# Longformer attention with two MLPs, one core: score banks filled up front, and new constants in the kernel's planner

## The chip, the cores and the metric

The kernel runs on one core of one Trainium2 chip. The metric is device time in microseconds (us), the median of several executions. TensorE is called PE here, VectorE DVE, ScalarE ACT, GpSimd POOL and SyncE SP.

## What is computed

```python
# local attention: 4 batches, 8 heads, 512 local and 32 global tokens, head size 64, window 32
s_ll = where(mask, scale * q_l @ k_l.T, -1e9)
out_l = sm(concat([scale * q_l @ k_g.T, s_ll])) @ concat([v_g, v_l])
out_g = sm(scale * q_g @ k_all.T) @ v_all
x = concat([out_g, out_l], axis=2)          # to [4*544 = 2176, 512]
h = x @ w_in                                # first MLP: 512 to 2048 to 512
x = (h * clip(h + 3, 0, 6) / 6) @ w_out
h = maximum(maximum(x @ w1, x @ w2), x @ w3)  # second MLP: 512 to 768 to 512
out = h @ w_out2
```

All of it is in float32. The large products split each operand into a high and a low part and make three products of them.

## The kernel before

The whole program is one list of steps. Each step (`op(...)`) names its engine, a cost in us, a due time, what it reads and writes and, for loads, the size in KB. `Plan.order()` walks a model of the chip, always taking the step that can start first (or, among those that can start within 0.02 us, the one due first), and writes the instructions out in the order found. On the chip every engine runs its instructions in that order, each waiting for its inputs; the planned times are not kept by anything. So a changed constant in the planner changes the order of instructions on PE, DVE, ACT, POOL and in SP's queue, and nothing else.

Attention runs per batch and pair of heads: `pair(b, pr, s0)`, 16 of them. The start `s0` of a pair, from which its due times count, grows by `STEPS[b]`. One pair loads Q, K (288 and 400 KB) and V (1024 KB) into rings of three buffers, makes the scores in two banks (L469: 64 small products), row maxima on DVE (L482), exponentials on ACT (L488), transposes (`flip`, L512), copies (L435), the product with V (`pv`, L523, output bank `o`), the division by the sums (L531), a second transpose (`xflip`, L538) and the split into high and low parts (`x_hi`, `x_lo`). Every second pair is followed by `globals_`, the attention of the global tokens (L576 to L628).

A score bank is not written everywhere by its scores, so each bank is first written whole by a product of ones, a *fill* (L419). Before, `full` holds six fills (four score banks, banks 6 and 7); the first scores wait for them, and the fifth score bank is filled after the first half of pair 0's scores.

Beside attention, 16 blocks of `w_in` are loaded through two buffers (`raw`, L664) and decoded on ACT, DVE and POOL (`decode`, `join`, L642 to L669). The first MLP's products (`first`, L695) fill PE's time between the steps of attention, as far as the attention output and the decoded weights are there. After the attention stage come the other products (L859, L983, L1138), with their own loads.

The planner's model has these terms that the change touches. Code for PE arrives in blocks of 256 instructions, the first border at `FIRST = 191`; when a border is passed, the next block but one is reckoned to arrive after `LATE` plus `SHARED` times the backlog of loads, at most 4 us. After an idle time of over 2 us, PE's steps count longer for 4 us (`cold`). A load of `kb` takes its turn in one pipe of 340 KB per us and lands 1.8 us later. `LOOK` says how far ahead the planner looks in sharing steps between ACT, DVE and POOL. `LAG` sets how early the weight loads of later stages may start.

In the last stage (L1120 and on), `single` and `double` take one or two blocks of 128 tokens. A `double` loads h twice (L1150, 384 KB, rows of 128 words), makes four sums of them on DVE or POOL (`wsum`, L677), splits them (L1160 and L677) and runs seven products through `quad` (L983), in which a copy of the first product's bank on ACT or DVE (`take`, L435) stands ahead of the third product.

Of the kernel before, what the change touches and what calls it, by code (L numbers as in the profile page):

```python
# [16 lines left out]
ALU = mybir.AluOpType  # L17
# [82 lines left out]
class Plan:  # L100
# [40 lines left out]
    def order(self):  # L141
# [15 lines left out]
        count, border, there, loads, cold = 0, FIRST, 0.0, [], -1e9  # L157
# [37 lines left out]
        while len(out) < len(self.ops):  # L195
            picks, wait, at = [], {}, {}
            for e, ops in cand.items():
                f = free.get(e, 0.0)
# [3 lines left out]
            for e, ops in cand.items():  # L202
# [5 lines left out]
                t0 = min(t for t, _ in ts)  # L208
# [21 lines left out]
            if o.eng == "PE":  # L230
                if FORM.get(o.what, "F") != form:
                    form = FORM.get(o.what, "F")
                    us += TURN
                if t - free.get("PE", 0.0) > 2.0 and t > COLD:
                    cold = t + 4.0
                if t < cold:
                    us += min(us, (cold - t) / 2)
                count += o.ni
                if count > border:
                    at_ = t + us * (1 - (count - border) / o.ni)  # L240
                    wait_ = max(0.0, there - at_)
                    at_, us = at_ + wait_, us + wait_
                    if wait_ > 0.2:
                        self.stalls.append((round(at_, 1), round(wait_, 1)))
                    if wait_ > 2.0:
                        cold = at_ + 4.0
                    behind = max([p - at_ for i, p in loads if i <= at_] + [0.0])
                    there, border = at_ + LATE + min(4.0, SHARED * behind), border + 256
# [30 lines left out]
COLD = 6.0  # L279
SPLIT = 2  # L280
LATE, SHARED = 2.473, 0.718
TS = "BC"
STEPS = (7.62, 8.87, 11.397, 7.881)
LAG = 124.236
# [4 lines left out]
LOOK = 1.25  # L289
# [6 lines left out]
def body(ctx, tc, q_n, k_n, v_r, w_in, w_o, w_3, w_4, out):  # L296
# [128 lines left out]
    full = [filled(bank) for bank in (*sbanks[:4], banks[6], banks[7])]  # L425
# [15 lines left out]
    def pair(b, pr, s0):  # L441
# [7 lines left out]
        for n, (t, src, cut, size) in enumerate(((Q, q_n, 256, NQ + SG), (K, k_n, 448, NK))):  # L449
            for i, (a, z) in enumerate(((0, cut), (cut, size)) if first_ else ((0, size),)):  # L450
                e, issue = ("ACT", nc.scalar) if first_ and n else ("SP", nc.sync)
                op(e, 0.45, lambda t=t, src=src, a=a, z=z, issue=issue: issue.dma_start(
                    out=t()[:, a:z], in_=src[b, pr][:, a:z]), s0 - 7.919 + i, w=[(t, i)] if first_ else [t],
                   kb=(z - a) / 2, rel=s0 - 15.079, what="qk"[n])
        op("SP", 0.5, lambda: nc.sync.dma_start(out=V(), in_=v_r[b, pr]), s0 - 4.432 + 5 * first_, w=[V], kb=1024, rel=s0 - 2.826, what="v")

        TB, NM, OB = [Buf(T["t"]) for _ in range(2)], Buf(T["nm"]), Buf(T["o"])
        for u, tiles in enumerate(((0, 1), (2, 3)) if first_ else (range(4),)):
# [18 lines left out]
            if not full[6:]:  # L477
                full.append(filled(sbanks[4], [head]))
# [27 lines left out]
        for hh in range(2):  # L506
            FB, pt = Buf(T["f"]), Buf(T["pt"])
            PT.append(pt)

            def flip(hh=hh, FB=FB):  # L510
                for i in range(4):
                    nc.tensor.transpose(FB()[:, 128 * i:128 * i + 128], TB[hh]()[:, i], ident)  # L512

            op("PE", 0.48, flip, s0 + 5.696 + hh, r=[(TB[hh], i) for i in range(4)], w=[FB, Buf(T["turn"])], what="flip", ni=8.2)
            op(AD, (0.585, 0.65), lambda e, pt=pt, FB=FB: copy(e, pt(), FB()), s0 + 5 + hh, r=[FB], w=[pt], what="flipped")
# [10 lines left out]
        op("PE", 0.95, pv, s0 + 3.515, r=PT + [V], w=[OB], what="pv", ni=129)  # L526
# [13 lines left out]
        op("PE", 0.48, xflip, s0 + 12.171, r=[OX], w=[XT], what="xflip", ni=8)  # L540
# [15 lines left out]
    def globals_(b, pr, g0):  # L556
# [7 lines left out]
        for a, ks in enumerate((GKEYS[0:2], GKEYS[2:3])):  # L564
# [14 lines left out]
            op("PE", (0.68, 0.3)[a], g_scores, g0 + 0.455, r=[Z[k] for Z in R for k in "QK"], w=[sg, (tg, "held")], what="g_scores", ni=8 * len(ks))  # L579
# [19 lines left out]
        for n, cs in enumerate((range(0, 4), range(4, 6))):  # L599
# [9 lines left out]
            op("PE", 0.11 * len(cs), g_flip, g0 + 3.512, r=[tg], w=[fb, Buf(T["turn"])], what="g_flip", ni=2 * len(cs))  # L609
# [13 lines left out]
        op("PE", 0.72, g_pv, g0 + 9.996, r=pts_g + [Z["V"] for Z in R], w=[og], what="g_pv", ni=96)  # L623
# [57 lines left out]
    def first(p, gs_, due):  # L681
# [28 lines left out]
        for g in gs_:  # L710
            store(p, g, Q[g], 0, 3, due)
            for a, b, o in ((3, 2, 2), (1, 3, 3), (1, 2, 1), (0, 1, 0)):
                op(DP if p in TS else "POOL", dp(n) if p in TS else pool(n), lambda e="POOL", g=g, o=o, a=a, b=b: tt(
                    e, q(g, o), q(g, a), q(g, b), ALU.subtract), due + 44.537, r=[(Q[g], a), (Q[g], b)], w=[(Q[g], o)], what="tsum",
                   two=True)
            store(p, g, Q[g], 3, 4, due)
# [9 lines left out]
    s = 4.158  # L726
    due1 = 40.0
    late = []
    for b in range(B + 1):
        if b < B:  # L730
            for pr in range(H // 2):
# [5 lines left out]
                if pr % 2:  # L737
                    late.append((b, pr, s + 3.453))
# [3 lines left out]
        if b == 0:  # L742
            for f in (g + NG * a for g in range(NG) for a in range(2)):
                src = w_in[:, f * 128:f * 128 + 128].rearrange("(k p) m -> p k m", p=128)
                k = 2 * (f % NG) + f // NG
                wi[f] = decode(src, "w", 22.156 + 1.579 * k, 11.396 + 1.115 * k)
# [344 lines left out]
    for p, i in (("P1", 0), ("R", 1), ("P2", 2), ("P3", 3), ("P5", 4), ("P6", 7), ("P7", 5), ("P4", 6)):  # L1091
# [3 lines left out]
           r=[(w4k, (k, i // 4)) for k in range(3)], w=[X4], kb=384, what="w4load", rel=TE - 30 - LAG)  # L1095
# [22 lines left out]
    def single(t0, due, t):  # L1118
# [4 lines left out]
        for i in range(2):  # L1123
            op("SP", 0.5, lambda i=i: nc.sync.dma_start(out=hl_()[:, i], in_=hd[:, 3 * i:3 * i + 2, t0:t0 + 128]), t - 20,
               r=rows(t0, (3 * i, 3 * i + 1)), w=[(hl, i)], kb=128, what="hload", rel=TE - 30 - LAG)
# [19 lines left out]
    def double(ts, due, t):  # L1145
# [3 lines left out]
        for i in range(2):  # L1149
            op("SP", 0.5, lambda i=i: nc.sync.dma_start(  # L1150
                out=blk(2 - 2 * i, 2).rearrange("p (k m) -> p k m", k=NH), in_=hd[:, :, ts[i]:ts[i] + 128]),
               t - 12, r=rows(ts[i]), w=[(W, 1 - i)], kb=384, what="hload")
# [76 lines left out]
```

## Time and profile before

| | us |
|---|---|
| median of 3 runs | 711.16 |
| lowest and highest | 710.18, 717.23 |
| profiled execution: time | 716.01 |
| profiled execution: span of the core | 714.2 |
| PE busy in the span | 696.9 (98%) |
| DVE, ACT, POOL busy | 526.7, 381.1, 128.9 |
| mean granted clock of PE | 0.993 |

The profile is of one execution, whose time is 1.8 us above its span. In the views, each line of a timeline has a start, a duration, the engine, the line of the kernel and the operation with its tiles; in brackets stands the idle time of the engine just before it and what ended that. A group "x64" is 64 instructions in a row.

### The profile page before, as it was taken

How to read it: one execution, taken by the hardware profiler on the slowest of the kernel's cores; microseconds unless marked ns; L12 is line 12 of the kernel's file. 1: busy time of each engine (PE TensorE's matmuls, PEld its weight loads, DVE VectorE, ACT ScalarE, POOL GpSimd, SP SyncE). 2: the span in 40 equal slices, each digit the busy share in tenths (PEclk: the TensorE clock that was granted, in tenths of full speed). 3: DMA queues.
4: the chain of work that ended last, by engine and by line, in shares of the span. 5: the costliest groups of instructions: out<-in, count | busy, mean ns of one | idle time of the engine just before them, and what ended most of it. 6: DMA issues, size and time to landing. Idle time of an engine off the chain costs nothing.

```text
span 714.2 us, 16046 instructions
## 1 busy us (share of the span) xinstructions
PE 696.9 (98%) x6380; PEld 619.8 (87%) x6380; DVE 526.7 (74%) x1114; ACT 381.1 (53%) x808; POOL 128.9 (18%) x163
## 2 busy tenths in 40 slices
PE   8799999999999999999999999999999999998998
PEld 5577878778888999988999998898999999997998
DVE  4688986657964575699867589998887876575781
ACT  6789887654332334565554366744454344254452
POOL 2137464200001343001010000011301320021210
PEclk9999999999999999999999999999999999999999
DMA  8599998715884765776576598001463371276542
GB/s 321 203 325 336 351 331 327 279 63 206 299 302 204 253 254 173 276 242 184 145 233 185 144 295 293 1 1 59 162 207 131 137 256 39 77 223 193 147 151 89
DMA packets 73147, 144.57 MB, mean 202 GB/s; under 512 B 4976, under 2 KB 43632, under 8 KB 70000
## 3 DMA queue, kind: packets, MB, share of 16 engines
q1 hardware_dynamic: 72784, 143.13, 59.0%
q8 instruction: 50, 0.82, 0.5%
q10 hardware_dynamic: 288, 0.41, 0.2%
q14 instruction: 25, 0.20, 0.1%
HBM read 98.04 MB, written 45.48 MB: 201 GB/s over the span
## 4 chain that ended last, share of the span: by engine, by line
PE 87%; DMA 6%; ACT 3%; DVE 2%; issue 1%; SPq 0%; POOL 0%; ACTq 0%; DVEq 0%
PE bank L983 33%; PE bank L695 23%; PE bank L859 22%; DMA raw<-in_w_in_dram 2%; DMA kr<-in_kn_dram 2%; PE o L523 1%; PE s L512 1%; PE s L469 1%; PE bank L1138 1%; DMA vr<-in_v_dram 1%; PE s L576 1%; PE s L620 1%; ACT t L488 1%; PE s L538 1%; DMA out_dram<-rf 1%
## 5 line engine op out<-in xcount | busy, mean ns | idle before, releaser
L695 PE MATMUL bank<-rx,rw 128*128 128x512 f32 (+1 forms) x960 | 198.0, 362 | 0.4 <-DVE rx L552 0.2
L695 PEld LDWEIGHTS bank<-rx,rw 128*128 128x128 f32 x960 | 161.7, 188 | 23.7 <-issue 1.2
L859 PE MATMUL bank<-rr,rw 128*128 128x320 f32 (+2 forms) x912 | 154.9, 331 | 0.7 <-DVE rr L677 0.6
L859 PEld LDWEIGHTS bank<-rr,rw 128*128 128x128 f32 x912 | 140.2, 188 | 14.8 <-DVE rr L677 1.8
L983 PE MATMUL bank<-rw,rr 128*128 128x256 f32 (+2 forms) x648 | 100.2, 302 | 0.1
L983 PEld LDWEIGHTS bank<-rw,rr 128*128 128x128 f32 x648 | 90.6, 188 | 5.0 <-ACT rf L435 0.7
L782 ACT CAST rr<-fw 128x1024 fp32r<-128x1024 f32 (+2 forms) x76 | 62.1, 820 | 53.6 <-PE bank L859 45.8
L677 DVE TENSOR_TENSOR rr<-fw,rr 128x1024 fp32r<-128x1024 f32 (+2 forms) x76 | 72.8, 964 | 23.6 <-ACT rr L782 22.8
L705 ACT ACTIVATE rq<-bank,three 128x512 f32<-128x512 f32 (+1 forms) x60 | 37.9, 635 | 48.6 <-PE bank L695 40.5
L677 POOL TENSOR_TENSOR rf<-rf 128x256 f32<-128x256 f32 (+2 forms) x34 | 34.3, 1020 | 142.6 <-DVE rf L652 40.8
L435 ACT COPY rf<-bank 128x256 f32<-128x256 f32 (+2 forms) x72 | 33.0, 465 | 47.6 <-PE bank L983 37.2
L707 DVE SCALAR_TENSOR_TENSOR rq<-rq,bank 128x512 f32<-128x512 f32 (+1 forms) x60 | 36.8, 618 | 29.1 <-ACT rq L705 28.7
L488 ACT ACTIVATE t<-t,nm 128x128 f32<-128x128 f32 x128 | 50.0, 394 | 13.4 <-DVE nm L482 13.2
L677 POOL TENSOR_TENSOR rq<-rq 128x256 f32<-128x256 f32 (+2 forms) x44 | 37.5, 853 | 108.3 <-DVE rq L677 82.4
L983 PE MATMUL bank<-rw,re 128*128 128x256 f32 (+2 forms) x369 | 54.4, 292 | 2.1 <-DVE bank L435 2.1
L983 PE MATMUL bank<-re,rr 128*128 128x512 f32 x222 | 54.9, 391 | 0.0
L983 PEld LDWEIGHTS bank<-rw,re 128*128 128x128 f32 x369 | 49.5, 188 | 3.7 <-DVE bank L435 2.3
L1077 DVE TENSOR_TENSOR rf<-rf,bank 128x320 f32<-128x320 f32 (+2 forms) x72 | 37.1, 530 | 14.3 <-PE bank L983 13.1
L983 PEld LDWEIGHTS bank<-re,rr 128*128 128x128 f32 x222 | 40.7, 188 | 8.0
L677 DVE TENSOR_TENSOR rf<-rf 128x256 f32<-128x256 f32 (+4 forms) x54 | 29.2, 572 | 7.2 <-DMA rf<-hd 7.1
L482 DVE CUSTOM_DVE_ANT_0 t<-s,mask 128x128 f32<-128x128 f32 x116 | 26.5, 285 | 10.6 <-PE s L469 10.6
L677 DVE TENSOR_TENSOR re<-rf,re 128x1024 fp32r<-128x1024 f32 (+4 forms) x20 | 26.5, 1330 | 3.9 <-ACT re L1160 3.9
(134 smaller groups left out, 970.2 us busy)
## 6 DMA issues: line engine op xcount, KB each, us to landing
vr<-in_v_dram SPq DMA_DIRECT2D x16, 1024.0 KB, 7.9
fw<-gsB SPq DMA_DIRECT2D x28, 512.0 KB, 4.8
raw<-in_w_dram SPq DMA_DIRECT2D x24, 512.0 KB, 3.9
fw<-gsC SPq DMA_DIRECT2D x28, 320.0 KB, 3.6
raw<-in_w_in_dram SPq DMA_DIRECT2D x16, 512.0 KB, 6.1
raw<-in_w_o_dram SPq DMA_DIRECT2D x16, 512.0 KB, 4.9
fw<-gsA SPq DMA_DIRECT2D x28, 256.0 KB, 2.9
gsB<-rq SPq DMA_DIRECT2D x6, 1024.0 KB, 5.1
```

The lines of the kernel that those rows point to most:

```text
L435: (nc.scalar.copy if eng == "ACT" else nc.vector.tensor_copy)(out=out, in_=in_)
L469: nc.tensor.matmul(SB[hh]()[QB * c:QB * c + QB, 128 * i + a:128 * i + z], lhsT=Q()[64 * hh:64 * hh + 64, QB * j:QB * j + QB], rhs=K()[64 * ...
L482: nc.vector.tensor_tensor_reduce(out=TB[hh]()[:, i], in0=SB[hh]()[:, 128 * i:128 * i + 128], in1=mask()[:, (i + 1) // 2 if i < 3 else 2], ...
L488: nc.scalar.activation(out=t, in_=t, func=ACTF.Exp, scale=-1.0, bias=NM()[:, 0, i, hh:hh + 1], accum_out=NM()[:, 1, i, hh:hh + 1])
L677: ENG[e].tensor_tensor(out=out, in0=a, in1=b, op=f)
L695: nc.tensor.matmul(ps()[:, 0:m], lhsT=w[:, i, k], rhs=xs(c)[:, j, k], start=(k == 0 and s == 0), stop=(k == KC - 1 and s == 2))
L705: op("ACT", us, lambda ps=ps, m=m, out=out: nc.scalar.activation(out=out(), in_=ps()[:, 0:m], func=ACTF.Relu, bias=three), -100, r=[ps], w ...
L707: op("DVE", us, lambda ps=ps, m=m, out=out: nc.vector.scalar_tensor_tensor(out=out(), in0=out(), scalar=6.0, in1=ps()[:, 0:m], op0=ALU.min ...
L782: op("ACT", act(n) + 0.01, lambda: nc.scalar.copy(out=out(0), in_=src()), due, r=r, w=[(w, "hi")], what=what + "_hi")
L859: nc.tensor.matmul(A[e]()[:, 0:n], lhsT=w[:, 2 * fp + f, u, e], rhs=r[:, v, f], start=(seed is None and fp + f + s == 0), stop=(fp == 3 an ...
L983: nc.tensor.matmul(bank()[:, 0:n], lhsT=w[:, u, k], rhs=r[:, v, k], start=(start and k + s == 0), stop=(k == K - 1 and s == 2), skip_group ...
L1077: op("DVE", dve(n), lambda q=q, src=src, mv=mv: nc.vector.tensor_tensor(out=mv(q)(), in0=mv(q)(), in1=src(), op=ALU.max), -200, r=[bank], ...
```

## The change

Seven fills (all five score banks and banks 6 and 7) stand ahead of the first scores, and the one behind them is gone. After the second half of pair 0's scores, two fills (`WARMERS = 2`) write the output bank `o`. In the planner, PE's steps except fills count up to double before 6.3 us (`cold` starts at `WARM`). The loads of w4 count as 500 KB instead of 384, those of h as 170 instead of 128 and as 560 instead of 384; the transfers themselves are the same. `LATE`, `SHARED`, `STEPS`, `LAG`, `LOOK` and the due and release times of Q, K, V, `flip`, `pv`, `xflip`, the global steps, the sums of the first MLP and the `w_in` loads have new values (those not in the excerpt: `g_scores` g0 + 0.455 to g0 + 0.071, `g_flip` g0 + 3.512 to g0 + 1.943, `g_pv` g0 + 9.996 to g0 + 5.183, the sums of the first MLP due + 44.537 to due + 48.004, the first s0 4.158 to 4.347, `globals_` s + 3.453 to s + 2.278). `COUNTED` is read nowhere in the diff.

```diff
-        count, border, there, loads, cold = 0, FIRST, 0.0, [], -1e9
+        count, border, there, loads, cold = 0, FIRST, 0.0, [], WARM
...
-                if t - free.get("PE", 0.0) > 2.0 and t > COLD:
+                if t - free.get("PE", 0.0) > 2.0 and t > WARM:
                     cold = t + 4.0
-                if t < cold:
+                if t < cold and o.what != "fill":
                     us += min(us, (cold - t) / 2)
...
-COLD = 6.0
+COUNTED = True
+WARM = 6.3
+WARMERS = 2
 SPLIT = 2
-LATE, SHARED = 2.473, 0.718
+LATE, SHARED = 2.304, 0.75
 TS = "BC"
-STEPS = (7.62, 8.87, 11.397, 7.881)
-LAG = 124.236
+STEPS = (7.844, 8.631, 11.405, 7.492)
+LAG = 127.749
...
-LOOK = 1.25
+LOOK = 0.745
...
-    full = [filled(bank) for bank in (*sbanks[:4], banks[6], banks[7])]
+    full = [filled(bank) for bank in (*sbanks, banks[6], banks[7])]
...
-                    out=t()[:, a:z], in_=src[b, pr][:, a:z]), s0 - 7.919 + i, w=[(t, i)] if first_ else [t],
-                   kb=(z - a) / 2, rel=s0 - 15.079, what="qk"[n])
-        op("SP", 0.5, lambda: nc.sync.dma_start(out=V(), in_=v_r[b, pr]), s0 - 4.432 + 5 * first_, w=[V], kb=1024, rel=s0 - 2.826, what="v")
+                    out=t()[:, a:z], in_=src[b, pr][:, a:z]), s0 - 12.857 + i, w=[(t, i)] if first_ else [t],
+                   kb=(z - a) / 2, rel=s0 - 14.853, what="qk"[n])
+        op("SP", 0.5, lambda: nc.sync.dma_start(out=V(), in_=v_r[b, pr]), s0 - 2.183 + 5 * first_, w=[V], kb=1024, rel=s0 - 3.098, what="v")
...
-            if not full[6:]:
-                full.append(filled(sbanks[4], [head]))
+            if first_ and u:
+                op("PE", 0.43 * WARMERS, lambda: [fill(OB()) for _ in range(WARMERS)], -100, after=[head], w=[OB], what="fill", ni=2 * WARMERS)
...
-            op("PE", 0.48, flip, s0 + 5.696 + hh, r=[(TB[hh], i) for i in range(4)], w=[FB, Buf(T["turn"])], what="flip", ni=8.2)
+            op("PE", 0.48, flip, s0 + 3.7 + hh, r=[(TB[hh], i) for i in range(4)], w=[FB, Buf(T["turn"])], what="flip", ni=8.2)
...
-        op("PE", 0.95, pv, s0 + 3.515, r=PT + [V], w=[OB], what="pv", ni=129)
+        op("PE", 0.95, pv, s0 + 2.373, r=PT + [V], w=[OB], what="pv", ni=129)
...
-        op("PE", 0.48, xflip, s0 + 12.171, r=[OX], w=[XT], what="xflip", ni=8)
+        op("PE", 0.48, xflip, s0 + 13.261, r=[OX], w=[XT], what="xflip", ni=8)
...
-                wi[f] = decode(src, "w", 22.156 + 1.579 * k, 11.396 + 1.115 * k)
+                wi[f] = decode(src, "w", 21.856 + 0.897 * k, 12.183 + 0.519 * k)
...
-           r=[(w4k, (k, i // 4)) for k in range(3)], w=[X4], kb=384, what="w4load", rel=TE - 30 - LAG)
+           r=[(w4k, (k, i // 4)) for k in range(3)], w=[X4], kb=500, what="w4load", rel=TE - 30 - LAG)
...
-               r=rows(t0, (3 * i, 3 * i + 1)), w=[(hl, i)], kb=128, what="hload", rel=TE - 30 - LAG)
+               r=rows(t0, (3 * i, 3 * i + 1)), w=[(hl, i)], kb=170, what="hload", rel=TE - 30 - LAG)
...
-               t - 12, r=rows(ts[i]), w=[(W, 1 - i)], kb=384, what="hload")
+               t - 12, r=rows(ts[i]), w=[(W, 1 - i)], kb=560, what="hload")
```

## Rows read from the trace of the kernel before

**Rows 1.** Busy time by stretch: us, engines, granted clock, DMA share, GB/s.

```profile
0.00:158.70 158.70, 147.40 (x3033) 116.03 (x3034) 113.43 (x464) 118.16 (x389) 56.19 (x96) 0.98 0.80 285
158.70:650.00 491.30, 490.43 (x2887) 445.92 (x2886) 375.70 (x597) 235.73 (x377) 65.51 (x63) 1.00 0.55 183
650.00:714.20 64.20, 59.09 (x464) 57.82 (x462) 37.58 (x53) 27.19 (x44) 7.24 (x4) 0.97 0.48 148
...
7.85:11.65 3.80, 3.75 (x76) 2.84 (x78) 1.80 (x11) 2.36 (x13) 0.20 (x1) 0.57 1.00 401
21.60:25.40 3.80, 3.68 (x65) 3.25 (x69) 2.16 (x6) 0.91 (x4) 0.00 (x0) 0.55 0.37 142
...
659.30:664.20 4.90, 4.89 (x28) 0.65 0.53 155
```

**Rows 2.** PE in order of time, 0 to 8 us: start, us, what.

```profile
1.05 1.89 PE L419 MATMUL s<-ones 128*128 128x512 bf16 x4 [1.05 <-DVE ones L318]
...
4.10 1.04 PE L469 MATMUL s<-kr,qr 64*32 64x96 f32 x32 [0.31 <-DMA kr<-in_kn_dram]
...
5.07 0.39 PE L419 MATMUL s<-ones 128*128 128x512 bf16 x1
...
5.39 0.65 PE L469 MATMUL bank<-kr,qr 64*32 64x128 f32 x32
...
7.90 1.59 PE L469 MATMUL s<-kr,qr 64*32 64x96 f32 x64 [1.86 <-DMA kr<-in_kn_dram]
```

**Rows 3.** PE's stops for issue, products before, and DMA queues from 18 us.

```profile
0.00:18.20 18.20, 14.76 (x348) 0.91 0.90 322
...
21.72 0.43 PE L523 MATMUL o<-vr,pt 128*32 128x64 f32 x15 [3.64 <-issue]
...
144.50 0.75 PE L620 MATMUL s<-vr,pt 128*32 128x64 f32 x35 [0.83 <-issue]
...
q8 instruction: 1, 0.02, 1.7%
```

**Rows 4.** SP's waits for w_in buffers, busy time by stretch, one PE wait.

```profile
SPq L664 <- DVE rq L652: 27.5, 7, 13.5
...
25.00:30.00 5.00, 4.66 (x177) 3.72 (x171) 4.17 (x14) 3.81 (x10) 0.80 (x2) 0.96 0.03 8
30.00:120.00 90.00, 87.20 (x1690) 69.19 (x1683) 74.58 (x287) 76.76 (x242) 43.91 (x58) 1.00 0.93 331
...
41.27 0.33 PE L512 MATMUL s<-ident,t 128*128 128x128 f32 x1 [1.26 <-ACT t L488]
```

**Rows 5.** V loads: median to landing, one issue, and its pv on PE.

```profile
vr<-in_v_dram SPq DMA_DIRECT2D x16, 1024.0 KB, 7.9
...
57.04 0.50 SPq L455 DMA_DIRECT2D vr<-in_v_dram  x1
...
65.32 1.10 PE L523 MATMUL o<-vr,pt 128*32 128x64 f32 x64 [0.31 <-DMA vr<-in_v_dram]
```

**Rows 6.** All engines in order of time, 654 to 660 us.

```profile
654.21 1.22 SPq L1150 DMA_DIRECT2D rf<-hd  x2
...
654.97 2.29 PE L983 MATMUL bank<-rw,re 128*128 128x256 f32 x18
...
656.83 2.09 DVE L677 TENSOR_TENSOR rf<-rf 128x384 f32<-128x384 f32 x4 [4.98 <-DMA rf<-hd]
...
658.84 0.42 DVE L435 COPY bank<-bank 128x256 f32<-128x256 f32 x1
...
659.31 1.51 PE L983 MATMUL bank<-rw,re 128*128 128x256 f32 x9 [2.06 <-DVE bank L435]
```

**Rows 7.** Loads by line: count, KB each, median us to landing.

```profile
rf<-hd SPq DMA_DIRECT2D x14, 384.0 KB, 4.6
...
rf<-w4d SPq DMA_DIRECT2D x8, 384.0 KB, 5.7
...
raw<-in_w_dram SPq DMA_DIRECT2D x24, 512.0 KB, 3.9
```

More of the change, by code (lines that the diff above doesn't have):

```diff
@@ L577, in g_scores @@
                                          tile_position=(0, 64 * m))
-            op("PE", (0.68, 0.3)[a], g_scores, g0 + 0.455, r=[Z[k] for Z in R for k in "QK"], w=[sg, (tg, "held")], what="g_scores", ni=8 * len(ks))
+            op("PE", (0.68, 0.3)[a], g_scores, g0 + 0.071, r=[Z[k] for Z in R for k in "QK"], w=[sg, (tg, "held")], what="g_scores", ni=8 * len(ks))
             for x, (_, at) in enumerate(ks):
@@ L607, in g_flip @@
                     nc.tensor.transpose(fb()[0:rows_g, 128 * j:128 * j + 128], tg()[:, at:at + rows_g], ident)
-            op("PE", 0.11 * len(cs), g_flip, g0 + 3.512, r=[tg], w=[fb, Buf(T["turn"])], what="g_flip", ni=2 * len(cs))
+            op("PE", 0.11 * len(cs), g_flip, g0 + 1.943, r=[tg], w=[fb, Buf(T["turn"])], what="g_flip", ni=2 * len(cs))
             e = ("ACT", "DVE")[n]
@@ L621, in g_pv @@
                                          start=(c == 0), stop=(c == 5), tile_position=(0, x))
-        op("PE", 0.72, g_pv, g0 + 9.996, r=pts_g + [Z["V"] for Z in R], w=[og], what="g_pv", ni=96)
+        op("PE", 0.72, g_pv, g0 + 5.183, r=pts_g + [Z["V"] for Z in R], w=[og], what="g_pv", ni=96)
         gx, xt = Buf(T["gx"]), Buf(T["s"])
@@ L713, in first @@
                 op(DP if p in TS else "POOL", dp(n) if p in TS else pool(n), lambda e="POOL", g=g, o=o, a=a, b=b: tt(
-                    e, q(g, o), q(g, a), q(g, b), ALU.subtract), due + 44.537, r=[(Q[g], a), (Q[g], b)], w=[(Q[g], o)], what="tsum",
+                    e, q(g, o), q(g, a), q(g, b), ALU.subtract), due + 48.004, r=[(Q[g], a), (Q[g], b)], w=[(Q[g], o)], what="tsum",
                    two=True)
@@ L723, in store @@
            r=[(Q, j) for j in range(k)], w=[(gk, (p, g, at))], kb=k * n / 2, what="gstore")
-    s = 4.158
+    s = 4.347
     due1 = 40.0
@@ L737, in body @@
                 if pr % 2:
-                    late.append((b, pr, s + 3.453))
+                    late.append((b, pr, s + 2.278))
                 s += STEPS[b]
```

## The prediction

> **What bounds the kernel now.** I read the span by stages first, because one share of busy time hides three different stages [rows 1]. In the attention stage (to 158.70 us) TensorE (PE) works 147.40 us, so it idles 11.30; in the middle, to 650 us, it idles 0.87; in the last 64.20 us it idles 5.11. PE is therefore the bound throughout, and a change of order can only win idle time or time at the lower clock. Almost all of both lies in three places. From 7.85 to 11.65 us the granted clock averages 0.57, from 21.60 to 25.40 it averages 0.55, and from 659.30 to 664.20 it averages 0.65, each time right after an idle stretch; a stretch at 0.5 runs at 1.2 GHz instead of 2.4 [rows 1]. The time that it costs is length times (1 - clock): 3.80 x 0.43 = 1.6 us, 3.80 x 0.45 = 1.7 us and 4.90 x 0.35 = 1.7 us.
>
> The second view is PE's own order of time at the start [rows 2], to see what each idle stretch waits for; the third is the place where PE stands without a visible cause [rows 3]; the fourth the loads and who holds SyncE's (SP's) queue [rows 4, 5]; the last is the gap near the end, engine by engine [rows 6].
>
> The sum is made against the profiled execution, 714.2 us of span and 716.01 us of time. The median of the runs shown is 711.16, 4.85 less, and no row says where those 4.85 us went; I come back to that below.
>
> **The change part by part.**
>
> *The seventh fill goes ahead of the first scores.* Before, six fills run first and the seventh stands after the first half of pair 0's scores: 0.39 us at 5.07, and the second half starts at 5.39 [rows 2]. Four fills take 1.89 us with one drain, so one costs about 0.43. Starting at 1.05, seven end about 1.05 + 7 x 0.43 = 4.06, plus a drain of some 0.2. The first scores start at 4.10 because they wait for the K load, so the added fill is hidden by that load: 0, between 0 and +0.2. The 0.3 us by which the second half of the scores comes earlier is worth nothing on the path: PE waits next for K of pair 1, until 7.90 [rows 2].
>
> *Two warming fills after the second half of the scores.* They write the output bank of pair 0, which nobody needs until its pv. They cost at most 2 x 0.43 = 0.86 us, half of it at the upper clock, in a hole of 1.86 us before 7.90 [rows 2], hence 0. Without that cover they would cost the 0.86. What they may bring is the clock of the stretch that follows: up to -1.6 by the product above. Neither a shorter hole nor its effect on the clock is in this trace; bounds 0 and -1.6. I take -0.6, nearer to nothing, because a hole of 1.0 to 1.4 us stays and because the work thus brought forward runs into the next stop.
>
> *That next stop, the planner's model of code loading (LATE, SHARED, the doubled first steps).* PE stands 3.64 us before 21.72 in the middle of pair 1's pv, for "issue" [rows 3], when 348 products have been recorded. Each has a weight load, so 696 instructions are recorded, and a few records may be missing; the planner puts its block borders at 191 + 2 x 256 = 703. A packet of the instruction queue moves in that stretch. A second such stop is 0.83 us at 144.50 [rows 3]. The Trainium skill, "Runtime: NRT & Kernel Launch", section on instruction fetch, says that crossing such a block is mostly hidden; by it the sum would have no such term. The row shows it not hidden, beside a full DMA load, so the row decides. The two warming fills bring 4 instructions more ahead of the border, so PE reaches it two matmuls earlier: nothing. New constants change where the planner expects the stop and what it lays around it. They do not shorten the stop. I take 0 for the first, with its 3.64 + 1.7 as the bound on the side of gain and 2 us for a longer one, and -0.4 for the second, half of its size.
>
> *Pace of the w_in loads, the look-ahead and the dues.* The w_in loads may now start at 12.2 and come every 0.5 us in the plan instead of every 1.1, and the order looks ahead 0.745 instead of 1.25. SP's queue holds a w_in load until DVE has finished with its buffer: 27.5 us in 7 waits, the longest 13.5, and from 25 to 30 us the DMA share is only 0.03. From 30 to 120 us it is 0.93 [rows 4]. The hole is paid back later: PE waits 1.26 at 41.27 [rows 4]. A faster decode can fill the hole, but the two buffers of raw words and DVE's order stay. Bounds: -1.26 if that wait goes, and +2.3 from new small waits elsewhere (what is left of the stage's 11.30 when the start, 1.05 and 0.31, and the stops of 1.86, 3.64, 1.26 and 0.83 are taken off). I take -0.6.
>
> *Q and K loads earlier, V later.* V's due goes from s0 - 4.432 to s0 - 2.183, 2.25 us later, while pv is due 1.14 earlier. V lands 7.9 us after issue, and the V issued at 57.04 is wanted at 65.32, where PE already waits 0.31 for it [rows 5]. I take +0.5; the bound is the rival below.
>
> *Higher prices for h and w4 loads at the end.* PE finishes 18 products that began at 654.97 and then stands 2.06 us to 659.31, waiting for a copy on DVE [rows 6]. That copy needs only the first nine products, but stands on DVE behind four sums that waited 4.98 us for an h load issued at 654.21. The copy came at 658.84; it could have run before the sums started at 656.83. So the planner had reckoned the loads earlier than they came. The change adds (560 - 384) / 340 = 0.52 us to each h load, 1.04 to a pair of them. The price of both h and w4 goes up, and the trace agrees in sign: 384 KB of h take 4.6 us and 384 KB of w4 take 5.7, against 3.9 for 512 KB of long rows [rows 7]. The Trainium skill, "DMA: Bandwidth & Descriptors", section Specifications, gives 512 bytes as enough for line rate; the h rows are 128 words, just that, so by it the new price is wrong and this term is 0. The row speaks against it.
> If the order on DVE turns over, the gap and the low clock behind it go: -2.06 - 1.7 = -3.76. Bounds: -3.76 and +1. I take the whole -3.76 as the likelier, at a little over even chance, since the sums began only about 0.7 us after the copy could.
>
> *Sum:* 0 - 0.6 - 0.4 - 0.6 + 0.5 - 3.76 = -4.9, from 716.0 to 711.1 for an execution like the profiled one. Against the median: the 4.85 us between the two executions must be idle or low-clock time of the same kinds, so an execution at the median has less to give. I halve the gain, -2.5, and forecast 708.5.
>
> **The rivals.**
> (A) *Nothing that binds moves.* The stop at the code border stays, the DVE order near the end turns out the same, small waits cancel. For it: the largest single loss (3.64 + 1.7) is not shortened by any edit. That gives 711 to 712. It is also the case that the change does not do what it says.
> (B) *All of it comes.* The clock holds from 7.85 on (-1.6), the wait at 41.27 goes (-1.3), the stop at 144.50 goes (-0.8), and the last gap goes (-3.8): -7.5 if the median execution has all of them, so 703.7. Against it: every one is a bound.
> (C) *V becomes the wait.* In the crowded stretch the V loads issued between 37 and 100 us have about as much lead as they need (8.28 us from 57.04 to 65.32, landing in 7.9). A lead that is shorter by the 2.25 of the due, less a slack of 0.4 to 1.7 us (I take 1.2 as the mean), makes PE wait about 1.0 at each of some seven pairs, +7, less the -2 of the other terms: 716. It decides from the point where V's slip is larger than its slack and no ready product of the first MLP stands by to fill the wait. For it: a DMA share of 0.93. Against it: PE takes such products when it can, and V's place in SP's queue is also set by its ring of three buffers.
>
> **How the numbers follow.** Forecast 0.45 (706 to 711), A 0.24 (710 to 713), B 0.18 (701 to 706), C 0.13 (713 to 720). The range 702 to 715.5 leaves out the lower edge of B and the upper half of C. A change of 1% is 7.1 us, about what a measurement of this kernel tells from none (its three runs span 7 us). Faster than 704.05: two thirds of B and a sliver of the forecast, 0.14. Slower than 718.3: the upper part of C, 0.06. Between: 0.80.
>
> **What would show it.** Right: seven fills in a row end near 4.2 us and the scores still start at 4.1 to 4.3; the granted clock between 8 and 11 us above 0.57; on DVE the copy ahead of the four sums near 656 us, PE without a gap there and at full clock behind it. The stop for issue stays near 21 us. Wrong: waits of pv for V between 40 and 100 us; a longer or another code stop in the attention stage; the gap of 2 us near the end at another place. The forecast falls if the attention stage ends later than 158.7, or if the runs at the median never had the last gap.

## The result and the profile after

The changed kernel takes 717.70 us (median of 20 runs, 713.88 to 720.22), the kernel before 711.07 (20 runs, 707.66 to 717.23): a ratio of 1.0082, with a 95% interval of 1.0064 to 1.0101. It is slower by 6.6 us, where 2.5 us less were forecast; the time lies above the range. The profiled execution of after took 719.86 us, its span is 718.1.

First the busy time of PE by stretch (us, PE busy with its products, granted clock, DMA share, GB/s), which answers to [rows 1, 3, 4]; the five lines that begin at 0.00 behind the first group end at PE's stops, which the next view explains.

```profile
0.00:158.70 158.70, 143.39 (x2904) 0.97 0.80 285
158.70:650.00 491.30, 488.90 (x2983) 1.00 0.54 181
650.00:718.10 68.10, 65.05 (x498) 1.00 0.48 151
...
0.00:21.40 21.40, 15.52 (x347) 0.92 0.87 327
0.00:41.30 41.30, 32.24 (x729) 0.92 0.76 272
0.00:47.40 47.40, 36.00 (x856) 0.93 0.77 277
0.00:104.60 104.60, 91.74 (x1872) 0.97 0.86 305
0.00:147.80 147.80, 132.53 (x2762) 0.98 0.84 299
...
147.80:152.00 4.20, 4.16 (x104) 0.62 0.61 199
...
30.00:120.00 90.00, 83.36 (x1573) 1.00 0.92 326
...
20.00:27.00 7.00, 5.29 (x145) 0.76 0.07 27
...
8.50:12.30 3.80, 3.75 (x77) 0.55 1.04 425
...
0.00:296.53 296.53, 280.33 (x3747) 0.98 0.72 259
296.53:715.05 418.52, 417.01 (x2637) 1.00 0.50 161
```

To 158.70 us PE has done 2904 products in place of 3033 [rows 1] and stood 15.3 us in place of 11.3. The first MLP's last product ends at 296.53; in the profile of before it ends at 289.35, so this part is 7.2 us longer. What follows it is shorter: 418.52 us against 711.15 - 289.35 = 421.80. The loss is made in attention and the first MLP, and some of it comes back later.

PE in order of time answers to [rows 2, 3, 5]:

```profile
1.05 2.32 PE L421 MATMUL s<-ones 128*128 128x512 bf16 x5 [1.05 <-DVE ones L320]
3.16 1.06 PE L421 MATMUL bank<-ones 128*128 128x512 bf16 x2
4.15 1.10 PE L471 MATMUL s<-kr,qr 64*32 64x96 f32 x32
...
5.76 0.60 PE L421 MATMUL o<-ones 128*128 128x512 bf16 x2
8.55 0.86 PE L471 MATMUL s<-kr,qr 64*32 64x96 f32 x28 [2.19 <-DMA kr<-in_kn_dram]
...
21.50 0.47 PE L525 MATMUL o<-vr,pt 128*32 128x64 f32 x18 [2.33 <-issue]
...
34.48 0.79 PE L471 MATMUL s<-kr,qr 64*32 64x96 f32 x40 [1.00 <-DMA kr<-in_kn_dram]
...
41.33 0.24 PE L525 MATMUL o<-vr,pt 128*32 128x64 f32 x1 [1.34 <-issue]
...
47.49 1.14 PE L578 MATMUL s<-kr,qr 128*64 128x192 f32 x12 [2.40 <-issue]
...
104.65 0.53 PE L525 MATMUL o<-vr,pt 128*32 128x64 f32 x21 [0.64 <-issue]
...
147.84 0.64 PE L622 MATMUL s<-vr,pt 128*32 128x64 f32 x27 [2.40 <-issue]
```

The start is as the plan wanted it: seven fills in a row, the scores at 4.15, the two warming fills in the hole before 8.55. What is new are five stops for issue, 2.33 + 1.34 + 2.40 + 0.64 + 2.40 = 9.1 us, where before had 3.64 + 0.37 + 0.83 = 4.8, and a wait for K at 34.48. In the first view the stops come after 347, 729, 856, 1872 and 2762 recorded products. The distances, 382, 127, 1016 and 890, are 3, 1, 8 and 7 times 128 products less up to 8, for records that may be missing or instructions of other kinds in between: with its weight load a product is two instructions, so the stops stand at borders of 256 instructions. Between 41.30 and 47.40 PE used up a whole such block with 3.76 us of work (36.00 - 32.24) and then stood 2.40; ahead of the stops at 41.33, 104.65 and 147.84 the last 127 products had taken 5.3, 6.3 and 4.8 us. Behind the last stop the granted clock was 0.62 for 4.20 us, which costs up to 4.20 x 0.38 = 1.6 us.

Behind the first MLP PE's largest waits are these (total, times, longest); the gap of [rows 6] is not among them:

```profile
PE bank L985 <- ACT rf L437: 0.9, 2, 0.6
```

And SP's longest waits of the first 160 us (total, times, longest), with three loads (count, KB, median us to landing), answering to [rows 4, 5, 7]. The w_in loads are held about as long as in the same stretch of before (42.2 us, 13 times), the hole in the DMA's work is still there (0.07 from 20 to 27 us, above), and V, h and w4 take 7.8, 4.4 and 4.7 in place of 7.9, 4.6 and 5.7:

```profile
SPq L666 <- DVE rq L654: 36.8, 14, 9.9
...
vr<-in_v_dram SPq DMA_DIRECT2D x16, 1024.0 KB, 7.8
...
rf<-hd SPq DMA_DIRECT2D x14, 384.0 KB, 4.4
...
rf<-w4d SPq DMA_DIRECT2D x8, 384.0 KB, 4.7
```

### The profile page after: what moved, and what is told of

Its sections match the earlier page's. It is cut to its first block, busy times and chain, and to the rows that moved or that the text cites. A ratio compares the mean times of both kernels' runs of the same rounds, so it can differ in the third digit from the quotient of the medians.

```text
span 718.1 us, 16048 instructions
## 1 busy us (share of the span) xinstructions
PE 697.3 (97%) x6382; PEld 619.9 (86%) x6382; DVE 528.6 (74%) x1113; ACT 382.2 (53%) x814; POOL 120.1 (17%) x158
## 4 chain that ended last, share of the span: by engine, by line
PE 82%; DMA 7%; ACT 4%; DVE 4%; issue 2%; SPq 0%; ACTq 0%; DVEq 0%
PE bank L985 32%; PE bank L861 23%; PE bank L697 17%; DMA raw<-in_w_o_dram 3%; DMA raw<-in_w_in_dram 2%; PE o L525 2%; PE bank L1140 2%; PE s L514 2%; PE s L471 2%; PE s L578 1%; DMA kr<-in_kn_dram 1%; PE s L540 1%; DMA raw<-in_w_dram 1%; PE s L622 1%; ACT t L490 1%
## 5 line engine op out<-in xcount | busy, mean ns | idle before, releaser
L437 ACT COPY rf<-bank 128x512 f32<-128x512 f32 (+2 forms) x71 | 32.3, 463 | 39.0 <-PE bank L985 28.6
L679 POOL TENSOR_TENSOR rf<-rf 128x256 f32<-128x256 f32 (+2 forms) x34 | 31.3, 933 | 127.5 <-DVE rf L654 55.9
L679 DVE TENSOR_TENSOR rf<-rf 128x384 f32<-128x384 f32 (+4 forms) x54 | 30.4, 595 | 3.2 <-DMA rf<-hd 3.2
L707 ACT ACTIVATE fw<-bank,three 128x320 f32<-128x320 f32 (+1 forms) x20 | 11.8, 592 | 29.9 <-PE bank L697 29.9
```

The source lines that it names most:

```text
L437: (nc.scalar.copy if eng == "ACT" else nc.vector.tensor_copy)(out=out, in_=in_)
L679: ENG[e].tensor_tensor(out=out, in0=a, in1=b, op=f)
L707: op("ACT", us, lambda ps=ps, m=m, out=out: nc.scalar.activation(out=out(), in_=ps()[:, 0:m], func=ACTF.Relu, bias=three), -100, r=[ps], w ...
```

## The experiments

All results in one place. "First" are the stops for issue up to 30 us, "later" those from there to the end of the first MLP, which the next column gives; both are of one profiled execution, whose own time stands under "profiled"; the median is of all runs, 4 to 20 of them. The profiled execution can lie far from the median: 4.9 us above it in before and 5.4 in e17 (the slowest of its ten), 4.5 below it in e1 (the fastest of its ten). So stops are set beside the profiled time and not beside the median. The ratio is to the kernel before on the same chip.

| kernel | median us | ratio, 95% interval | profiled | first | later | end of first MLP |
|---|---|---|---|---|---|---|
| before | 711.07 | | 716.01 | 3.64 | 1.20 | 289.35 |
| before again (e9) | 712.32, one run | | 712.32 | 3.25 | 2.61 | 287.27 |
| after | 717.70 | 1.0082 [1.0064, 1.0101] | 719.86 | 2.33 | 6.78 | 296.53 |
| load prices alone (e1) | 711.38 | 0.9984 [0.9954, 1.0014] | 706.92 | 2.27 | 0.34 | 284.83 |
| after, old load prices (e4) | 717.05 | 1.0084 [1.0049, 1.0119] | 718.72 | 2.36 | 5.82 | 295.28 |
| dues and code constants alone (e2) | 717.09 | 1.0077 [1.0048, 1.0107] | 716.89 | 3.23 | 1.98 | 292.62 |
| fills and doubled first steps (e3) | 720.44 | 1.0120 [1.0081, 1.0159] | 720.98 | 2.60 | 3.10 | 295.53 |
| fills alone (e13) | 721.72 | 1.0127 [1.0059, 1.0194] | 720.26 | 3.58 | 3.05 | 292.87 |
| doubled first steps alone (e14) | 720.45 | 1.0108 [1.0078, 1.0138] | 717.93 | 2.85 | 2.36 | 292.22 |
| before, borders shifted (e5) | 712.74 | 1.0022 [0.9998, 1.0046] | 716.38 | 3.62 | 4.55 | 293.36 |
| after, borders shifted (e6) | 720.05 | 1.0098 [1.0065, 1.0130] | 719.54 | 2.37 | 6.42 | 296.93 |
| after, old dues (e12) | 717.71 | 1.0088 [1.0051, 1.0125] | 714.71 | 2.22 | 1.04 | 291.79 |
| the same, block price 5.0 (e7) | 713.22 | 1.0019 [0.9999, 1.0039] | 715.47 | 2.08 | 1.10 | 290.35 |
| after, block price 5.5 (e8) | 716.41 | 1.0051 [1.0024, 1.0077] | 716.25 | 2.09 | 0 | 292.81 |
| fills alone, block price 5.25 (e15) | 713.19 | 1.0003 [0.9968, 1.0038] | 716.40 | 1.63 | 0 | 291.20 |
| after, half of V (e10) | 711.82 | 0.9996 [0.9965, 1.0027] | 709.67 | 1.81 | 0.35 | 286.35 |
| before, half of V (e11) | 709.50 | 0.9969 [0.9946, 0.9991] | 710.56 | 3.64 | 0 | 286.92 |
| first steps alone, half of V (e16) | 716.82 | 1.0045 [1.0026, 1.0065] | 716.76 | 2.80 | 0.67 | 291.65 |
| fills alone, half of V (e17) | 714.55 | 1.0025 [0.9995, 1.0055] | 719.98 | 4.98 | 0.35 | 291.92 |

**The change taken apart.** Four kernels came first: before with the new load prices alone; before with the new dues, steps, lag, look and code constants; before with the fills and the doubled first steps; and after with the old prices.

```diff
# e1: before with these, and e4: after without them
-  kb=384, what="w4load"      +  kb=500
-  kb=128, what="hload"       +  kb=170
-  kb=384, what="hload"       +  kb=560
```

> The kernel before with the new prices of the h and w4 loads alone (500, 170, 560 KB). Theory (the prices turn the order near the end, as the changed kernel's trace shows no gap there): the attention stage is as before and the last stage loses the 2.06 us gap and the 1.7 us of low clock, so about 711.1 - 3.8 = 707.3. Rival (the gap went because everything reached that place at another time): no change, 711.

> The kernel before with the new dues, STEPS, LAG, LOOK, LATE and SHARED, but with the old fills, the old treatment of the first steps and the old load prices. Theory (the new dues lay short products together, PE uses up its code blocks faster than they come, and stops): the first MLP ends some 5 to 7 us later than before, 716 to 718, with several stops for issue of 0.5 to 2.5 us. Rival (the fills and the doubled first steps did it): 711.

> The kernel before with the seven fills ahead, the two warming fills and the doubled first steps, and all else as before. Theory (the dues did it): 711 to 712. Rival (the fills and the doubled first steps set another order from the first microseconds on, and that order has the stops): 716 to 718.

> The changed kernel with the old load prices. Theory: the gap near the end is back, so the changed kernel's 717.7 + 3.8 = 721.5. Rival (the gap depends on the arrival time, not on the prices): 717.7.

The prices, on which most of the forecast gain hung, are worth -1.1 us with an interval from -3.3 to +1.0 alone, and after loses as much with the old ones as with the new. e1 has PE's order of before up to the end of the first MLP, e4 that of after. That gives three executions of the one order and two of the other; here are that stretch and the 3.8 us behind the hole at the start, of e1 and of e4:

```profile
0.00:284.83 284.83, 277.10 (x3745) 0.99 0.74 270
...
8.60:12.40 3.80, 3.80 (x80) 0.64 1.04 411
```

```profile
0.00:295.28 295.28, 278.17 (x3747) 0.99 0.72 260
...
8.50:12.30 3.80, 3.52 (x92) 1.00 1.04 418
```

By the ratios the dues alone lose 5.5 us, fills and doubled first steps together 8.5. The load prices leave the order of the first 641 us alone; all other parts re-plan the attention stage. Later the second group was taken apart as well:

```diff
# e13, fills alone (before has neither WARMERS nor the last step)
-    full = [filled(bank) for bank in (*sbanks[:4], banks[6], banks[7])]
+    full = [filled(bank) for bank in (*sbanks, banks[6], banks[7])]
...
-            if not full[6:]:
-                full.append(filled(sbanks[4], [head]))
+            if first_ and u:
+                op("PE", 0.43 * WARMERS, lambda: [fill(OB()) for _ in range(WARMERS)], -100, ...)
# e14, doubled first steps alone
-        count, border, there, loads, cold = 0, FIRST, 0.0, [], -1e9
+        count, border, there, loads, cold = 0, FIRST, 0.0, [], WARM
...
-                if t - free.get("PE", 0.0) > 2.0 and t > COLD:
+                if t - free.get("PE", 0.0) > 2.0 and t > WARM:
...
-                if t < cold:
+                if t < cold and o.what != "fill":
```

> Before with the fills alone: all banks filled ahead of the first scores and two fills of O's bank behind the second scores; the planner's doubled first steps, prices, dues and code constants stay before's. Theory (any re-planned order loses the places that before's code borders had): 716 to 721, first MLP's last product 292 to 297 us, stops for issue up to there 7 to 11 us. Rival 1 (the fills cost nothing and the doubled first steps make the loss): 710 to 713. Rival 2 (the fills themselves cost, by their own work at the start): the loss lies ahead of 15 us, as fewer products recorded up to the first stop's time than in before.

> Before with the planner's doubled first steps alone (it counts TensorE's steps up to 10 us at up to double their length), every instruction that is issued being the same as in before and in another order. Theory (re-planning is the loss, whichever entry causes it): 715 to 720, first MLP's last product at 291 to 296 us. Rival (the doubled steps do no harm, the fills make the loss): 710 to 713.

Each loses alone: 1.27% and 1.08%. e14 issues the same 6380 products and the same 309 loads and stores on SP's queue as before, in another order; about a dozen of some 2085 steps on DVE, ACT and POOL also change their engine, since the planner shares them out anew. So a new order with the same work costs 7.7 us here (5.5 to 9.8 by the interval). The losses of the parts do not add: by the ratios 9.0, 7.7 and 5.5 us apart, 5.8 together (6.6 by the medians). What e13 loses is not the fills' own time: its second pair's scores start at 8.12, within the 7.90 to 8.60 us of the three executions of before's order.

**Does the profile belong to the order?** The kernel before was run once more.

> The kernel before once more, unchanged, for one profile. Theory: the places of TensorE's stops for issue stay (348, 2383 and 2764 recorded products), since the order is the same, and their lengths vary by a microsecond or so; the first MLP's last product ends within 2 us of the 289.35 us of before's profile, and the span's end is 710 to 716. Rival (a profile says nothing of the order, each execution draws its own stops): other places, a first MLP that ends 4 us or more from 289.35. Of the gap at 656 to 660 us, which was there in one execution of this tail and absent in another, no forecast: if it is absent here, it belongs to the execution; if present, to the order.

```profile
0.00:287.27 287.27, 276.10 (x3745) 1.00 0.74 268
...
8.30:12.10 3.80, 3.43 (x85) 1.00 1.03 416
```

```profile
20.90 0.43 PE L523 MATMUL o<-vr,pt 128*32 128x64 f32 x15 [2.70 <-issue]
...
58.84 1.10 PE L469 MATMUL s<-kr,qr 64*32 64x96 f32 x64 [1.05 <-issue]
...
142.52 0.75 PE L620 MATMUL s<-vr,pt 128*32 128x64 f32 x35 [0.97 <-issue]
...
657.18 1.33 PE L983 MATMUL bank<-rw,re 128*128 128x256 f32 x9 [1.46 <-DVE bank L435]
```

The large stop (20.90, before at 21.72) and the one at 142.52 (144.50) are the same; three others, 0.55 at 14.41, 1.05 at 58.84 and 0.59 at 97.20, are new, at borders too, and before's 0.37 at 126.12 is gone. So an order fixes where the borders are, and the execution which of them is late. The gap of [rows 6] is there with 1.46 in place of 2.06 us. But in the next experiment (e5), whose tail is in the order of before to the last instruction, it is absent: the products run from 658.47 without a break. In a third one with that tail (e11) it is 0.63.

**The borders moved.** Forty products of 32 columns, written to the output bank `o` that nobody reads yet, were put into the hole before 8 us; everything else stays in its order (the step of the scores also lists `o` among what it writes, a line not shown), and every later border falls 40 products earlier.

```diff
+                for _ in range(SHIFT if first_ and u else 0):
+                    nc.tensor.matmul(OB()[:, 0:32], lhsT=ones, rhs=ones[:, 0:32], start=True, stop=True)
```

> The kernel before with 40 very short products of ones (32 columns) put into PE's idle hole between pair 0's scores and pair 1's. Every other instruction of every engine keeps its place in the order. The only thing that changes is where the borders of PE's code blocks fall, 40 products earlier. Theory A (stops for issue come at code borders, and the order before was one whose borders fell well): with about 5.5 us for a block, the steps between the shifted borders leave some 7 us more of stops, so 716 to 719, with stops at new places, 40 products earlier in the count. Rival (stops come from the loads' traffic or from the order itself): 711 to 712, stops at the same steps.

> The changed kernel with the same 40 short products in the same hole, and nothing else moved. Theory A: about 7 us more of stops by the same reckoning, 722 to 726; the stop between the global pv and the next global scores near 46 us falls 40 products earlier, inside the global pv or the scores. Rival: 717 to 718.

```profile
18.84 0.99 PE L526 MATMUL o<-vr,pt 128*32 128x64 f32 x55 [2.31 <-issue]
...
41.83 1.27 PE L623 MATMUL s<-vr,pt 128*32 128x64 f32 x37 [2.02 <-issue]
...
113.14 0.43 PE L526 MATMUL o<-vr,pt 128*32 128x64 f32 x15 [1.72 <-issue]
...
658.47 1.70 PE L986 MATMUL bank<-rw,re 128*128 128x256 f32 x13
```

The stops moved with the borders and came to 8.2 us in the profiled execution (two more, 1.31 at 27.95 and 0.81 at 70.62, are not shown). That execution took 716.38 us and is the slowest of its ten, so its stops say little of the median, which rose by 1.6 us (-0.1 to +3.3 by the interval), less than the 5 to 8 that I had expected. In after the shift made +1.1 us by the ratios, within the intervals, where I had expected 4 to 8. So the places of the borders alone, in an order that is otherwise kept, are not shown to cost anything, and at most some 3 us in before.

**Longer blocks in the plan.** The planner's constants let a block arrive 2.3 to 2.5 us after the border before it, plus part of the backlog. In three kernels (e7, e8 and e15; e12 is the one to compare e7 with) this is a constant of 5.0 to 5.5 us instead, so that the planner lays long products where a block of short ones would run out.

```diff
-                    there, border = at_ + LATE + min(4.0, SHARED * behind), border + 256
+                    there, border = at_ + CODE, border + 256
```

> The changed kernel with all dues, STEPS, LAG and LOOK of before, and with the arrival of a code block reckoned as a constant 5.0 us after the border before it, in place of LATE and SHARED. Theory A (the planner's price for a code block was too low, so it laid short products together): fewer stops than in the kernel before and the new load prices beside it, 708 to 710. Rival (any other order than the one before is worse, whatever the price): 717 to 720, as the fills alone gave.

> The changed kernel with one line changed: a code block is reckoned to come a constant 5.5 us after the border before it. Theory A: the stops for issue fall from 9 us to 4 or 5, 713 to 715. Rival (the loss is that K and V come later): 717 to 718 with the same waits for K.

> The kernel after with all of before's due times, steps, lag and look, that is before with the fills ahead, the doubled warming fills, the load prices and the two code constants of after, and without the constant price of a code block that the kernel of 713.2 us had on top. It tells what that price did. Theory (the fills ahead and the planner's doubled first steps re-plan the order, and its code borders fall where blocks are used up within 4 us): 717 to 721 as the kernel with fills alone (720.4), first MLP's last product at 293 to 297 us, stops for issue up to there 8 us or more. Rival (the old dues were enough to bring the old order's luck back, and the block price did nothing): 711 to 714, stops under 6 us.

> The fills alone, as in the first of these three, and a constant price of a code block: the planner takes each block to have arrived 5.25 us after the border before it, in place of 2.473 us and 0.718 of the queued loads (at most 4 us). Theory (the loss is where the code borders fall, and a planner that spreads short products over at least that time gets it back): 4 to 7 us below the fills alone, 710 to 714, stops for issue up to the first MLP's last product under 6 us. Rival (the price only moves the waits elsewhere): within 2 us of the fills alone.

e15 against e13 is one line of difference, and 8.5 us in the medians. In e13 PE's largest stops were these (with 0.56, 0.26 and 0.45 they make 6.6):

```profile
20.98 0.47 PE L524 MATMUL o<-vr,pt 128*32 128x64 f32 x17 [3.02 <-issue]
...
78.20 0.74 PE L696 MATMUL bank<-rx,rw 128*128 128x512 f32 x2 [0.84 <-issue]
113.88 1.89 PE L696 MATMUL bank<-rx,rw 128*128 128x512 f32 x7 [1.50 <-issue]
```

and of e15's waits these are the ones to compare (total, times, longest):

```profile
PE o L525 <- DMA vr<-in_v_dram: 3.1, 3, 1.3
...
PE o L525 <- issue: 1.6, 2, 0.9
```

The stops fell from 6.6 to 1.6 us and part came back as waits for V (0.7 to 3.1). With old dues the price of 5.0 is worth 4.5 us (e12 to e7), though the two profiled executions do not show where. In e12 I had expected stops of 8 us or more; there are 3.3, fewer than in before, in an execution that was 3.0 us faster than e12's median. In after with its new dues 5.5 takes every later stop away and gives back only 2.2 us (1.0082 to 1.0051, intervals that overlap). In their place stand waits on DVE (for `ox` 2.9 us, in after 0.2):

```profile
PE s L541 <- DVE ox L534: 2.9, 3, 1.5
...
PE s L623 <- issue: 2.1, 1, 2.1
PE s L515 <- DVE nm L506: 1.4, 1, 1.4
```

None of these kernels is faster than the one before, clear of the noise; load prices alone equal it.

**The rings relieved.** Code, K and V come through the same 16 DMA engines, busy 0.92 from 30 to 120 us. Half of each V load was left out with every order unchanged (both heads of a pair then use the first head's V): 16 x 512 KB less.

```diff
-        ... nc.sync.dma_start(out=V(), in_=v_r[b, pr]) ...
+        ... nc.sync.dma_start(out=V()[:, 0], in_=v_r[b, pr][:, 0]) ...
-                                         rhs=V()[:, hh, 4 * i + c], ...
+                                         rhs=V()[:, 0, 4 * i + c], ...
...
-                        ... rhs=Z["V"]()[0:k, hh, j], ...
+                        ... rhs=Z["V"]()[0:k, 0, j], ...
```

> The kernel after, with half of each V load left out (both heads of a pair use the first head's V, so the output is another one); the order of every queue and engine is unchanged. Theory (the stops for issue at code borders are long because the packets of code share the rings with some 40 us of queued loads, and after's order uses its blocks up faster than they are refilled): with 16 x 512 KB less in the rings the stops up to the end of the first MLP fall from 9.1 us to under 5, that stage ends 5 to 8 us earlier (289 to 291.5), and the median falls to 709 to 713. Rival (the stops are the price of a crossing, whatever the rings hold): stops stay at 8 to 10 us, the median above 715. Against the next kernel, before with the same half left out, after would stand at +2 us or less by the theory, at +6 by the rival.

> The kernel before, with half of each V load left out (both heads of a pair use the first head's V); order of every queue unchanged. Theory: its stops for issue up to the end of the first MLP are 4.8 us; with the rings emptier 2 to 3 us are left, and the median falls by 2 to 4 us, to 707 to 709.5, less than after falls by the same edit (5 to 8). Rival (stops do not hang on the rings, but waits for loads do): both kernels fall alike, by the few waits for V and K.

> The doubled first steps alone, with half of each V load left out (both heads of a pair use the first head's V); every queue and engine in the order of the kernel with 720.45 us. There the profile had 5.2 us of stops for issue, 2.8 of waits for K and 1.7 for V up to the end of the first MLP. Theory (what a re-planned order loses is time in which code, K or V, whichever the order puts last, comes late through full rings): the median falls by 6 to 9 us, to 711.5 to 714.5, and the waits for issue, K and V together from 9.7 us to under 5. Rival (the re-planned order loses by itself, by its dependences on DVE and ACT): a fall of 2 to 3 us as in the kernel before (2.2), to 717.5 or more.

> The fills alone, with the same half of each V load left out; order as in the kernel with 721.7 us, whose profile had 6.6 us of stops for issue, 1.3 of waits for K and 0.7 for V up to the end of the first MLP. Theory (full rings): the median falls by 6 to 10 us, to 712 to 716, stops for issue under 3 us. Rival (the order's own dependences): a fall of 2 to 3 us, to 718.5 or more.

(The 40 us of queued loads in the first of these stands in no trace: in after the loads of the first 160 us land at most 12.0 us after their issue.) After fell by 5.9 us, before by 2.2; the distance between the two shrank from 6.6 to 2.3. After's stops for issue are now two:

```profile
19.39 0.47 PE L525 MATMUL o<-vr,pt 128*32 128x64 f32 x18 [1.81 <-issue]
...
139.60 0.64 PE L622 MATMUL s<-vr,pt 128*32 128x64 f32 x27 [0.35 <-issue]
```

and the gap near the end, in before with half of V:

```profile
654.79 1.33 PE L983 MATMUL bank<-rw,re 128*128 128x256 f32 x9 [0.63 <-DVE bank L435]
```

In all four pairs the later stops fell under 0.7 us (6.78 to 0.35, 1.20 to 0, 2.36 to 0.67, 3.05 to 0.35); the first ones, near 20 us, did not (2.33 to 1.81, 3.64 to 3.64, 2.85 to 2.80, 3.58 to 4.98). Beside before with the same V, by the ratios, after keeps 1.9 of 5.8 us, the fills alone 4.0 of 9.0, the first steps alone 5.4 of 7.7. So relief of the rings takes two thirds of after's loss, over half of the fills' and less than a third of the first steps', whose run came out between the theory and the rival. By the intervals only the fall of after's loss, 3.9 us with some 3 either way, is clear of the noise; the fills' 5.0 and the first steps' 2.3 are not. And the edit does not single out code: after's waits for K fell with it from 3.2 to 1.0 us. In e17, against the theory, 5.3 us of stops stayed.

## Why the prediction was wrong

The sum treated each constant as a local edit. Each of them but the load prices re-plans the whole order of the attention stage, and that order was worth more than all the terms together. By the five executions of the two orders: the first MLP ends at 289.35, 287.27 and 284.83 (mean 287.2) in the old, at 296.53 and 295.28 (295.9) in the new, 8.8 us later. Idle time is 11.30, 11.17 and 7.73 (10.1) against 16.20 and 17.11 (16.7), 6.6 of the 8.8; stops for issue are 4.84, 5.86 and 2.61 (4.4) against 9.11 and 8.18 (8.6), 4.2 of it, and waits for K 3.9 in place of 2.3, some 1.5 of it. The remaining 2.2 us are PE time: behind a hole or a stop of 1.9 to 3.6 us the granted clock was at half (1.2 GHz; 0.50 from 148.80 to 152.20 us in after) for some 3.4 us three times in after and twice in e4, against twice, never and once in the old order, at about 1.7 us each. Behind the first MLP after and e4 take 418.5 and 418.6 us, before and e9 421.8 and 420.2; but e5 and e11, which have before's order there, take 418.2 and 418.8. So what after seemed to win there is not shown to be its order's. The whole profiled executions of the five differ by 7.5 us (719.3 against 711.8), the medians by 6.6.

- *Seventh fill and warming fills: 0, as forecast.* The scores start at 4.15, and K ends the hole at 8.55 (7.90 to 8.60 in the old order). The -0.6 for the clock behind it found no support: the hole got no shorter (2.19 us, before 1.86), and the granted clock of those 3.8 us was 0.55 in after and 1.00 in e4, which starts in the same order, and 0.57, 1.00 and 0.64 in the three executions of the old one.
- *"That next stop": the step that failed.* I took 0 for the length of the stop near 21 us; by the means of the five executions it got 0.7 us shorter (2.3 for 3.1). For the one other stop I took -0.4; the later stops came to 6.3 us in place of 1.4, +4.9, so +4.2 in all, where my one bound on the side of loss was 2, for a longer first stop. I looked at the stops that before had and not at the borders it has anyway, of which each can become one. "Another code stop in the attention stage" was my own sign of being wrong, and after has four of them, before two. The Trainium skill, "Runtime: NRT & Kernel Launch", section on instruction fetch, calls the crossing mostly hidden; here stops of 0.2 to 4.4 us at one to six borders of every execution are not. This step accounts for after and not for the parts alone: the profiled executions of e12, e2 and e14 have 3.3, 5.2 and 5.2 us of stops, like the old order's 2.6 to 5.9, and take 714.71, 716.89 and 717.93 us, 3.0 to 6.2 above the mean of the old order's three (by the ratios they lose 6.3, 5.5 and 7.7). There the step that failed is the wider one, a new order priced at nothing but its local terms.
- *Pace of w_in, look-ahead and dues: wrong in sign.* I took -0.6 with +2.3 as the bound. SP's waits for w_in and the hole in the DMA's work stayed, a K wait of 1.00 came at 34.48 (1.91 at 35.47 in e4), and the dues alone lose 5.5 us (3.4 to 7.6 by the interval).
- *V later, +0.5, and rival C.* No pv waits for V in after, neither 0.5 us nor rival C's 7. C had the side right and the mechanism wrong; V waits of over 1 us show in e5 (1.2), e14 (1.7) and e15 (3.1) only.
- *Load prices and last gap, -3.76.* Mis-sized: prices alone gave -1.1, unresolved, with an interval that ends at -3.3. In four executions with the same tail the gap is 2.06, 1.46, 0.63 and 0 us (before, e9, e11, e5), so it was no property that a median execution has in full. After has no gap there, but neither has e4 with the old prices, and its later stages are as short (713.90 - 295.28 = 418.62).
- *Halving against the median.* The 4.85 us between the profiled execution and the median were right to distrust: executions of one order differ by 4.5 us at the end of the first MLP alone.

What stays open: why the first stop stays at 1.8 to 4.4 us with half of V (the DMA share in it was 1.03 in before and 0.04 in after with half of V, where it still took 1.81); and how the losses of e2, e12 and e14 are made up: the stops do not account for them, and halving V, tried on e14 of these, took less than a third. That an order can lose by its own dependences on DVE and ACT was not tested by itself.

## What to carry to other kernels

Where one list scheduler writes the whole order, a changed cost is a new kernel: price the edit by a run with the order changed and the work equal before arguing any of its terms. Count every place where an order can lose time (here each border of code, with blocks of short products and the rings full ahead of it), not only those where the old one did. And take two or three profiles of the kernel before: a gap that one of them lacks is no gain to bank.

## What the runs showed of the hardware

PE's code was late at borders of 256 instructions: a block of 127 products with 3.76 us of work was followed by a stop of 2.40 us, in a stretch with a DMA share of 0.92; blocks that lasted 4.8 to 6.3 us were followed by stops of 0.64 to 2.40 as well. Which borders are late differs between executions of one order: 3.64, 0.37 and 0.83 us in one, 2.27 and 0.34 in another. With V's traffic halved the stops beyond 30 us fell from between 1.2 and 6.8 us per execution to between 0 and 0.7, so their length hangs on the traffic beside them; the first stop did not shrink so. A stop of 2.40 us at 147.84 was followed by a granted clock of 0.62 for 4.20 us, another of 2.40 at 47.49 in the same execution by 1.00. One and the same order was granted 0.55 behind a hole of 2.19 us in one execution and 1.00 behind a hole of 2.50 in another. And the 20 runs of before span 9.6 us, so one profile does not stand for the median.
